# Sharing a PSUM slot between values and transposed values, adding a fourth first-layer slot, and giving pair copies and an eighth of the squares to GpSimd

## The chip, the cores and the metric

The kernel runs on one core of a Trainium2 chip. The metric is the device time of one execution in microseconds (us). A profile also gives the span, the time between the first and the last instruction, which is about 1.7 us shorter than the time (before: span 247.69, time of that run 249.41).

A ratio below is the mean time of a kernel's fast runs over the mean of the fast runs of the kernel before in the same rounds, so it is not quite the ratio of the medians that are quoted beside it. The brackets after a ratio are its 95% interval.

The engines: TensorE (PE in the profile; PEld are its weight loads), VectorE (DVE), ScalarE (ACT), GpSimd (POOL). PSUM, where matmuls write, is used here as two pools: three large slots of two banks and two small slots of one bank.

## The reference, cut to what matters

```python
# attention in chunks of 32 queries; keys: 8 memory keys, 16 left, 32 own, 8 right
for c in range(nc):
    k_full = concatenate([mem_k, k[:, :, l_start:r_end]]);  v_full likewise
    a = exp(scale * q_c @ k_full.T - max);  a = a / sum(a)
    out[:, :, chunk c] = a @ v_full
# then, with x = attention output as (3072 tokens, 512):
h = x @ w_in                              # 512 -> 2048, "first layer"
g = h + sin(alpha * h)**2 / alpha         # alpha per column of w_in
y = g @ w_out                             # 2048 -> 512, "second layer"
```

There are 4 batches of 768 tokens, 8 heads of 64.

Of the kernel before, what the change touches and what calls it, by code (L numbers as in the profile page):

```python
# [9 lines left out]
P = 128  # L10
# [35 lines left out]
def kernel(  # L46
# [154 lines left out]
    nc.scalar.copy(memv_st[64:72], memv_f[64:72])  # L201
# [23 lines left out]
    def pair_up(src, hp):  # L225
        pr = blk.tile([P, 6, 2, D], BF, name="pr")
        nc.vector.tensor_copy(
            pr[:].rearrange("p r e d -> p e r d"), src[:, 2 * hp:2 * hp + 2]
        )
        return pr  # L230
# [52 lines left out]
    def pv(b, j, pt):  # L283
# [15 lines left out]
        return x_blk  # L299

    def xt(xT, j, x_blk):
        xtp = smp.tile([P, KT, QW], BF, name="xtp", tag="sm")
        for kt in range(KT):
            nc.tensor.transpose(  # L304
                xtp[:, kt, :], x_blk[:, 2 * kt:2 * kt + 2, :].rearrange("p e d -> p (e d)"), ident[0:QW, 0:QW]
            )
        nc.vector.tensor_copy(xT[:, :, QW * j:QW * j + QW], xtp[:])  # L307

    def burst(b, stream, shares, lag):
# [3 lines left out]
        for s in range(NJ + lag + 1):  # L313
# [5 lines left out]
            stream.take(n // 2)  # L319
            if 0 <= s - lag < NJ:  # L320
                xbl[s - lag] = pv(b, s - lag, ptl.pop(s - lag))
            stream.take(n - n // 2)
            if 0 <= s - lag - 1 < NJ:
                xt(xT, s - lag - 1, xbl.pop(s - lag - 1))
# [3 lines left out]
    def l1(i, ft, xT, gT, dve_sq):  # L328
        hT = big.tile([P, 2, 512], F32, name="hT", tag="big")
        for kt in range(KT):  # L330
            for hf in range(2):
                nc.tensor.matmul(  # L332
                    hT[:, hf, 0:HALF],
# [5 lines left out]
        nc.scalar.activation(u[:], hT[:, :, 0:HALF], ACTF.Sin, scale=alpha_sb[:, ft:ft + 1])  # L339
        s2 = mlp.tile([P, 2, HALF], F32, name="s2")  # L340
        if dve_sq:
            nc.vector.tensor_tensor(out=s2[:], in0=u[:], in1=u[:], op=ALU.mult)  # L342
        else:
            nc.scalar.activation(s2[:], u[:], ACTF.Square)  # L344
        nc.vector.scalar_tensor_tensor(  # L345
            out=gT[:, ft, :].rearrange("p (e c) -> p e c", e=2),
            in0=s2[:], scalar=inv_alpha[:, ft:ft + 1], in1=hT[:, :, 0:HALF],
            op0=ALU.mult, op1=ALU.add,
        )

    def l2(i, gT, last=False):
        for s in range(NSUB):
            o = smp.tile([P, d_model], F32, name="o", tag="sm")
            for ft in range(FT):
                nc.tensor.matmul(  # L355
                    o[:], gT[:, ft, P * s:P * s + P], w_out_sb[:, ft, :],
                    start=(ft == 0), stop=(ft == FT - 1),
                )
                if ft < FT - 1:
                    yield False  # L360
            o_sb = mlp.tile([P, d_model], F32, name="o_sb")
            if s % 2 == 0:
                nc.vector.tensor_copy(o_sb[:], o[:])  # L363
            else:
                nc.scalar.copy(o_sb[:], o[:])  # L365
            nc.sync.dma_start(out[S * i + P * s:S * i + P * s + P, :], o_sb[:])
            yield True


    prs = [pair_up(kq[n % 2], n // 2) for n in range(2)]  # L370
    for n in range(2 * HP):
        (t_k if n % 2 == 0 else t_q)(prs[n], n // 2)
        spin(2)
        if n + 2 < 2 * HP:
            prs.append(pair_up(kq[n % 2], (n + 2) // 2))
    mt = smp.tile([P, HP, 32], BF, name="mt", tag="sm")
    for hp in range(HP):
        nc.tensor.transpose(mt[:, hp, :], memk_bf[0:32, 2 * hp:2 * hp + 2, :].rearrange("p e d -> p (e d)"), ident[0:32, 0:32])
    nc.vector.tensor_copy(memkT[:], mt[:])
    put_memk(0)  # L380
    put_memv(0)
# [13 lines left out]
    for i in range(B):  # L395
        gT = gp.tile([P, FT, S], BF, name="gT")
        last = i == B - 1
        at_ft = {1: 0, 3: 1, 5: 2, 7: 3, 9: 4, 11: 5, 13: 6, 14: 7}
# [15 lines left out]
        for ft in range(FT):  # L414
            dve_sq = ft % 3 == 1 if i == 0 else ft % 4 == 3
# [4 lines left out]
            l1(i, ft, xT, gT, dve_sq)  # L420
# [3 lines left out]
        if not last:  # L424
# [9 lines left out]
            else:  # L434
                xT = burst(i + 1, stream, (5, 6, 7, 7, 7, 7, 7, 7, 7, 7), 1)
# [37 lines left out]
```

## The kernel before: the parts that the change touches

Each batch goes through an attention of eight blocks of 96 queries, a first layer of 16 tiles (ft), and a second layer of 6 sums. The second layer of one batch is cut into single matmuls (`stream.take(n)` emits up to n of them: it stops where a sum ends and leaves the rest to the next take) that fill TensorE during the next batch's attention and first layer. Batch 0 has nothing to fill with, so its attention has a dummy matmul per block (`spin(1)`).

```python
big = tile_pool(name="big", bufs=3, space=PSUM)      # large slots: sc, ot, hT, z (dummy)
smp = tile_pool(name="smp", bufs=2, space=PSUM)      # small slots: o, xtp, tt_a

def pair_up(src, hp):                                # puts the two heads of a pair side by side
    nc.vector.tensor_copy(pr, src[:, 2*hp:2*hp+2])

def pv(b, j, pt):                                    # values of block j
    ot = big.tile(...)
    # 8 matmuls ot <- pt, vw ; rinv = 1/sum ; x_blk = ot * rinv       (VectorE)
    return x_blk

def xt(xT, j, x_blk):                                # transposed values
    xtp = smp.tile([P, KT, QW], BF, name="xtp", tag="sm")
    # 4 transposes xtp <- x_blk
    nc.vector.tensor_copy(xT[:, :, QW*j:QW*j+QW], xtp[:])

def burst(b, stream, shares, lag):                   # one attention
    for s in range(NJ + lag + 1):
        ptl[s] = qk_exp(s)                           # 8 score matmuls into sc, 3 exponentials
        if b == 0: spin(1)                           # one dummy matmul into a large slot z
        stream.take(n // 2);   xbl[s-lag] = pv(...)
        stream.take(n - n//2); xt(xT, s-lag-1, xbl.pop(s-lag-1))

def l1(i, ft, xT, gT, dve_sq):                       # one first-layer tile
    hT = big.tile(...)                               # 8 matmuls
    u  = sin(alpha * hT)                             # ScalarE
    s2 = u * u                                       # VectorE if dve_sq, else ScalarE
    gT[:, ft] = s2 * inv_alpha + hT                  # VectorE, scalar_tensor_tensor ("STT")
...
for c in range(8): load_w_in(c)                      # all these DMAs are issued by GpSimd,
kq_next = load_qk(1)                                 # in this order
for c in range(4): load_w_out(c)
load_v_all(1)                                        # four loads: values of batch 1
xT = burst(0, stream, (), 2)
...
dve_sq = ft % 3 == 1 if i == 0 else ft % 4 == 3
at_ft = {1: 0, 3: 1, 5: 2, 7: 3, 9: 4, 11: 5, 13: 6, 14: 7}   # key/query transposes, batches 1, 2
```

The softmax here doesn't subtract the row's maximum and nothing guards it: scores larger than these inputs give would overflow.

## Time and profile before

The time before was 250.03 us (median of 3, 249.28 to 250.76). Stages overlap little on TensorE, so I cut the span at the first weight load of each stage, and the end at the end of the last weight load.

| stage (before) | starts at | lasts |
|---|---|---|
| attention 0 | 17.50 | 13.00 |
| first layer 0 and the transposes for batch 1 | 30.50 | 34.67 |
| attention 1 | 65.17 | 16.15 |
| first layer 1 | 81.33 | 31.88 |
| attention 2 | 113.21 | 24.54 |
| first layer 2 | 137.75 | 31.95 |
| attention 3 | 169.70 | 24.67 |
| first layer 3 and last second layer | 194.37 | 49.14 |
| end (last copy and output) | 243.50 | 4.19 |

A timeline line of the profile reads: start, length, engine, line of the kernel, operation, output<-inputs, shapes, count, and in brackets the idle time before it with what ended that idle time. Two pieces of the chain that ended last (start, length, what), between 24 and 32 us, show what led through attention 0 before:

```profile
23.82 1.21 ACT pt L276 x3
31.15 1.31 PE hT L332 x7
```

The chain goes from ScalarE's exponentials over TensorE and VectorE to the first layer's matmuls; no DMA and no GpSimd instruction stands in this part of the chain.

### The profile page before, as it was taken

The numbers are of one execution on the slowest core, as the hardware profiler recorded it, in microseconds if no ns is written. First come the engines' busy times: TensorE is split into PE (matmuls) and PEld (weight loads), VectorE is DVE, ScalarE is ACT, GpSimd is POOL, SyncE is SP. The second block draws the span as 40 slices with busy tenths as digits, with TensorE's granted clock in tenths as the row PEclk, the third lists the DMA queues.
The fourth block names the chain that finished last, engine by engine and source line by source line (L and its number), as shares of the span: only waits on it lengthen the run. The fifth ranks groups of instructions, "written<-read, shape, count | busy, mean of one in ns | idle before, by whom it ended". The sixth has DMA issues, their size and how long they took to land.

```text
span 247.7 us, 4445 instructions
## 1 busy us (share of the span) xinstructions
PE 221.4 (89%) x1769; PEld 122.5 (49%) x1769; DVE 147.0 (59%) x282; ACT 172.3 (70%) x261; POOL 48.1 (19%) x70
## 2 busy tenths in 40 slices
PE   6788788999989998987899997988899999989994
PEld 2345445555445565653455564653455455543441
DVE  3257958897059677675546577776456176575110
ACT  3679678898895797999462798899653687891000
POOL 8899955100900000180000000000000000000000
PEclk9799999999999999999999999999999999999999
DMA  7999999999999700299911101001111101101122
GB/s 79 168 120 70 153 195 204 207 199 118 167 214 154 72 3 12 42 195 143 144 53 42 45 0 42 3 0 42 44 45 43 45 0 42 43 4 42 47 83 85
DMA packets 53709, 21.11 MB, mean 85 GB/s; under 512 B 36280, under 2 KB 50616, under 8 KB 53688
## 3 DMA queue, kind: packets, MB, share of 16 engines
q0 software_dynamic: 47616, 14.40, 72.7%
q1 hardware_dynamic: 6072, 6.43, 8.8%
q8 instruction: 14, 0.23, 0.4%
q14 instruction: 7, 0.06, 0.1%
HBM read 28.91 MB, written 6.29 MB: 142 GB/s over the span
## 4 chain that ended last, share of the span: by engine, by line
PE 55%; ACT 25%; DVE 11%; issue 5%; DMA 2%; SPq 1%; DVEq 0%; ACTq 0%
PE o L355 27%; PE hT L332 18%; ACT u L339 8%; ACT s L344 6%; ACT pt L276 5%; DVE gT L345 3%; PE ot L289 3%; DVE x_blk L294 2%; DMA memv_f<-in_mem_v_dram 2%; PE sc L267 2%; ACT o_sb L365 2%; ACT L276 2%; DVE s L342 2%; PE xtp L304 1%; ACT kTi L244 1%
## 5 line engine op out<-in xcount | busy, mean ns | idle before, releaser
L355 PE MATMUL o<-w_out_sb,gT 128*128 128x512 bf16 x384 | 100.2, 379 | 4.2 <-ACT o_sb L365 1.7
L332 PE MATMUL hT<-xT,w_in_sb 128*128 128x384 bf16 x512 | 91.7, 326 | 4.0 <-DVE gT L345 3.6
L345 DVE SCALAR_TENSOR_TENSOR gT<-s,inv_alpha,hT 128x768 bf16<-128x768 f32 x64 | 64.4, 1013 | 38.2 <-ACT s L344 35.9
L339 ACT ACTIVATE u<-hT,alpha_sb 128x768 f32<-128x768 f32 x64 | 57.3, 897 | 17.1 <-PE hT L332 16.8
L332 PEld LDWEIGHTS <-w_in_sb 128*128 128x128 bf16 x512 | 49.3, 98 | 39.2 <-issue 6.2
L355 PEld LDWEIGHTS <-gT 128*128 128x128 bf16 x384 | 33.9, 97 | 33.3 <-issue 3.9
L276 ACT ACTIVATE pt<-sc,biasm 128x256 bf16<-128x256 f32 x96 | 37.4, 490 | 13.7 <-PE sc L267 13.5
L344 ACT ACTIVATE s<-u 128x768 f32<-128x768 f32 x47 | 39.6, 843 | 1.5
L365 ACT COPY o_sb<-o 128x512 f32<-128x512 f32 x12 | 7.0, 582 | 30.2 <-PE o L355 30.1
L294 DVE TENSOR_TENSOR x_blk<-ot,rinv 96x512 bf16<-96x512 f32 x32 | 22.0, 686 | 1.1
L293 DVE RECIPROCAL rinv<-ot 96x8 f32<-96x8 f32 x32 | 6.4, 199 | 21.6 <-PE ot L289 21.5
L342 DVE TENSOR_TENSOR s<-u 128x768 f32<-128x768 f32 x17 | 16.2, 955 | 2.7 <-ACT u L339 2.6
L289 PEld LDWEIGHTS <-pt 128*128 128x128 bf16 x256 | 11.8, 97 | 10.9 <-ACT pt L276 3.6
L363 DVE COPY o_sb<-o 128x512 f32<-128x512 f32 x12 | 8.2, 687 | 14.4 <-PE o L355 14.3
L171 PE MATMUL z<-zeros 128*128 128x512 bf16 x37 | 14.1, 468 | 2.2 <-DVE zeros L165 1.3
L289 PE MATMUL ot<-vw,pt 128*128 128x65 bf16 x256 | 13.0, 193 | 3.4 <-ACT pt L276 3.0
L307 DVE COPY xT<-xtp 128x384 bf16<-128x384 bf16 x32 | 11.2, 351 | 3.1 <-PE xtp L304 2.0
L267 PE MATMUL sc<-qT,kTi 64*128 64x96 bf16 x256 | 11.0, 205 | 1.8 <-DVE kTi L159 0.8
L304 PEld LDWEIGHTS <-x_blk 96*128 96x128 bf16 x128 | 8.4, 97 | 8.1 <-DVE x_blk L294 2.2
L115 POOL DMA_DIRECT2D k_bf<-in_k_dram x3 | 2.8, 922 | 49.1 <-DVE kTi L250 49.1
L304 PE MATMUL xtp<-ident,x_blk 96*128 96x96 bf16 x128 | 10.8, 206 | 1.3 <-DVE x_blk L294 1.0
L258 PEld LDWEIGHTS <-pr 128*128 128x128 bf16 x96 | 6.5, 99 | 9.2 <-issue 2.3
(53 smaller groups left out, 142.4 us busy)
## 6 DMA issues: line engine op xcount, KB each, us to landing
out_dram<-o_sb SPq DMA_DIRECT2D x24, 256.0 KB, 2.0
k_bf<-in_k_dram POOLq DMA_DIRECT2D x3, 768.0 KB, 8.2
q_bf<-in_q_dram POOLq DMA_DIRECT2D x3, 768.0 KB, 12.0
vw<-in_v_dram POOLq DMA_DIRECT2D x6, 384.0 KB, 15.7
w_in_sb<-in_moe_w_in_dram POOLq DMA_DIRECT2D x8, 256.0 KB, 7.8
w_out_sb<-in_moe_w_out_dram POOLq DMA_DIRECT2D x4, 512.0 KB, 19.0
k_bf<-in_k_dram POOLq DMA_DIRECT2D x4, 192.0 KB, 6.0
q_bf<-in_q_dram POOLq DMA_DIRECT2D x4, 192.0 KB, 6.4
```

The lines of the kernel that those rows point to most:

```text
L171: nc.tensor.matmul(z[:], zeros[:, 0:P], zeros[:])
L267: nc.tensor.matmul(sc[:, e, QW * hp:QW * hp + QW], kTi[64 * e:64 * e + 64, hp, 104 * j:104 * j + P], qT[64 * e:64 * e + 64, hp, QW * j:QW ...
L276: nc.scalar.activation(pt[:, 0:H * QW].rearrange("p (g e c) -> p e g c", g=4, e=2)[:, :, :, 32 * m:32 * m + 32], sc[:, :, 0:4 * QW].rearra ...
L289: nc.tensor.matmul(otv[:, h // 4, h % 4, :], pt[:, QW * h:QW * h + P], vws[b % 2][:, h, j, 0:D + 1])
L294: nc.vector.tensor_tensor(out=x_blk[:].rearrange("p (g e) d -> p g e d", g=2), in0=otv[0:QW, :, :, 0:D], in1=rv.unsqueeze(3).to_broadcast( ...
L304: nc.tensor.transpose(xtp[:, kt, :], x_blk[:, 2 * kt:2 * kt + 2, :].rearrange("p e d -> p (e d)"), ident[0:QW, 0:QW])
L332: nc.tensor.matmul(hT[:, hf, 0:HALF], w_in_sb[:, kt, P * ft:P * ft + P], xT[:, kt, HALF * hf:HALF * hf + HALF], start=(kt == 0), stop=(kt ...
L339: nc.scalar.activation(u[:], hT[:, :, 0:HALF], ACTF.Sin, scale=alpha_sb[:, ft:ft + 1])
L342: nc.vector.tensor_tensor(out=s2[:], in0=u[:], in1=u[:], op=ALU.mult)
L344: nc.scalar.activation(s2[:], u[:], ACTF.Square)
L345: nc.vector.scalar_tensor_tensor(out=gT[:, ft, :].rearrange("p (e c) -> p e c", e=2), in0=s2[:], scalar=inv_alpha[:, ft:ft + 1], in1=hT[:, ...
L355: nc.tensor.matmul(o[:], gT[:, ft, P * s:P * s + P], w_out_sb[:, ft, :], start=(ft == 0), stop=(ft == FT - 1),)
```

## The change

Its intent: take the pair copies off VectorE and a third of the squares off ScalarE, use GpSimd, which is busy for 19% of the span, and free the small PSUM slots so that a second-layer sum need not wait for the last one's copy. Of ScalarE's 47 squares, 8 go to GpSimd and 7 to VectorE. The core of the diff:

```diff
-    def pair_up(src, hp):
+    def pair_up(src, hp, eng=None):
-        nc.vector.tensor_copy(
+        (eng or nc.gpsimd).tensor_copy(            # the first ones still on VectorE
...
-    def xt(xT, j, x_blk):
-        xtp = smp.tile([P, KT, QW], BF, name="xtp", tag="sm")
+    def xt(xT, j, x_blk, ot):                      # ot: the values' slot of the same block
+        xtp = ot[:].bitcast(BF)[:, 0, 640:640 + KT * QW].rearrange("p (k c) -> p k c", k=KT)
...                                                  # burst: takes in three parts, not two, and on past a sum's end
-    def l1(i, ft, xT, gT, dve_sq):
-        hT = big.tile([P, 2, 512], F32, name="hT", tag="big")
+    def l1(i, ft, xT, gT, sq, split=False):
+        if split:                                  # the "fourth slot": the two small ones
+            hts = [smp.tile([P, 512], F32, name="hs", tag="sm") for _ in range(2)]
...                                                  # sine and STT in halves if split
+            (nc.vector if sq == "D" else nc.gpsimd).tensor_tensor(
+                out=s2[:], in0=u[:], in1=u[:], op=ALU.mult)
...
-        at_ft = {1: 0, 3: 1, 5: 2, 7: 3, 9: 4, 11: 5, 13: 6, 14: 7}
+        at_ft = {2 * n: n for n in range(8)}
-            dve_sq = ft % 3 == 1 if i == 0 else ft % 4 == 3
+            sq = ("ADAPADAD" if i == 0 else "ADAPADAD")[ft % 8]
-            l1(i, ft, xT, gT, dve_sq)
+            l1(i, ft, xT, gT, sq, i == 0 and ft % 4 == 3)
-                xT = burst(i + 1, stream, (5, 6, 7, 7, 7, 7, 7, 7, 7, 7), 1)
+                xT = burst(i + 1, stream, (9, 9, 7, 6, 6, 6, 6, 6, 6, 5), 1)
```

In "ADAPADAD" A is ScalarE, D VectorE, P GpSimd. Cut here: the last second-layer sum comes out in two halves, and the steps that prepare the memory keys and values come in another order at the start.

More of the change, by code (lines that the diff above doesn't have):

```diff
@@ L200 @@
     nc.scalar.copy(memk_bf[:], memk_f[:])
-    nc.scalar.copy(memv_st[64:72], memv_f[64:72])
     for j in range(NJ):
@@ L298, in pv @@
         )
-        return x_blk
-    def xt(xT, j, x_blk):
-        xtp = smp.tile([P, KT, QW], BF, name="xtp", tag="sm")
+        return x_blk, ot
+    def xt(xT, j, x_blk, ot):
+        xtp = ot[:].bitcast(BF)[:, 0, 640:640 + KT * QW].rearrange("p (k c) -> p k c", k=KT)
         for kt in range(KT):
@@ L306, in xt @@
             )
-        nc.vector.tensor_copy(xT[:, :, QW * j:QW * j + QW], xtp[:])
+        nc.vector.tensor_copy(xT[:, :, QW * j:QW * j + QW], xtp)
     def burst(b, stream, shares, lag):
@@ L318, in burst @@
                 spin(1)
-            stream.take(n // 2)
+            stream.take(n // 3, True)
             if 0 <= s - lag < NJ:
                 xbl[s - lag] = pv(b, s - lag, ptl.pop(s - lag))
-            stream.take(n - n // 2)
+            stream.take((n + 1) // 3, True)
             if 0 <= s - lag - 1 < NJ:
-                xt(xT, s - lag - 1, xbl.pop(s - lag - 1))
-        return xT
-    def l1(i, ft, xT, gT, dve_sq):
-        hT = big.tile([P, 2, 512], F32, name="hT", tag="big")
+                xt(xT, s - lag - 1, *xbl.pop(s - lag - 1))
+            stream.take((n + 2) // 3, True)
+        return xT
+    def l1(i, ft, xT, gT, sq, split=False):
+        if split:
+            hts = [smp.tile([P, 512], F32, name="hs", tag="sm") for _ in range(2)]
+        else:
+            hT = big.tile([P, 2, 512], F32, name="hT", tag="big")
+            hts = [hT[:, 0], hT[:, 1]]
         for kt in range(KT):
@@ L332, in l1 @@
                 nc.tensor.matmul(
-                    hT[:, hf, 0:HALF],
+                    hts[hf][:, 0:HALF],
                     w_in_sb[:, kt, P * ft:P * ft + P],
@@ L338, in l1 @@
         u = mlp.tile([P, 2, HALF], F32, name="u")
-        nc.scalar.activation(u[:], hT[:, :, 0:HALF], ACTF.Sin, scale=alpha_sb[:, ft:ft + 1])
+        if split:
+            for hf in range(2):
+                nc.scalar.activation(
+                    u[:, hf], hts[hf][:, 0:HALF], ACTF.Sin, scale=alpha_sb[:, ft:ft + 1])
+        else:
+            nc.scalar.activation(u[:], hT[:, :, 0:HALF], ACTF.Sin, scale=alpha_sb[:, ft:ft + 1])
         s2 = mlp.tile([P, 2, HALF], F32, name="s2")
-        if dve_sq:
-            nc.vector.tensor_tensor(out=s2[:], in0=u[:], in1=u[:], op=ALU.mult)
-        else:
-            nc.scalar.activation(s2[:], u[:], ACTF.Square)
-        nc.vector.scalar_tensor_tensor(
-            out=gT[:, ft, :].rearrange("p (e c) -> p e c", e=2),
-            in0=s2[:], scalar=inv_alpha[:, ft:ft + 1], in1=hT[:, :, 0:HALF],
-            op0=ALU.mult, op1=ALU.add,
-        )
+        if sq == "A":
+            nc.scalar.activation(s2[:], u[:], ACTF.Square)
+        else:
+            (nc.vector if sq == "D" else nc.gpsimd).tensor_tensor(
+                out=s2[:], in0=u[:], in1=u[:], op=ALU.mult)
+        gv = gT[:, ft, :].rearrange("p (e c) -> p e c", e=2)
+        for hf in range(2):
+            if split:
+                nc.vector.scalar_tensor_tensor(
+                    out=gv[:, hf], in0=s2[:, hf], scalar=inv_alpha[:, ft:ft + 1],
+                    in1=hts[hf][:, 0:HALF], op0=ALU.mult, op1=ALU.add)
+            elif hf == 0:
+                nc.vector.scalar_tensor_tensor(
+                    out=gv, in0=s2[:], scalar=inv_alpha[:, ft:ft + 1],
+                    in1=hT[:, :, 0:HALF], op0=ALU.mult, op1=ALU.add)
     def l2(i, gT, last=False):
@@ L353, in l2 @@
             o = smp.tile([P, d_model], F32, name="o", tag="sm")
-            for ft in range(FT):
-                nc.tensor.matmul(
-                    o[:], gT[:, ft, P * s:P * s + P], w_out_sb[:, ft, :],
-                    start=(ft == 0), stop=(ft == FT - 1),
-                )
-                if ft < FT - 1:
-                    yield False
-            o_sb = mlp.tile([P, d_model], F32, name="o_sb")
-            if s % 2 == 0:
-                nc.vector.tensor_copy(o_sb[:], o[:])
-            else:
-                nc.scalar.copy(o_sb[:], o[:])
-            nc.sync.dma_start(out[S * i + P * s:S * i + P * s + P, :], o_sb[:])
+            end = last and s == NSUB - 1
+            o_sb = mlp.tile([P, d_model], F32, name="o_sb")
+            row = S * i + P * s
+            if end:
+                oh = [o, smp.tile([P, d_model], F32, name="o", tag="sm")]
+                for c in range(2):
+                    cs = slice(256 * c, 256 * c + 256)
+                    for ft in range(FT):
+                        nc.tensor.matmul(
+                            oh[c][:, 0:256], gT[:, ft, P * s:P * s + P], w_out_sb[:, ft, cs],
+                            start=(ft == 0), stop=(ft == FT - 1),
+                        )
+                    if c == 0:
+                        nc.scalar.copy(o_sb[:, cs], oh[c][:, 0:256])
+                    else:
+                        nc.vector.tensor_copy(o_sb[:, cs], oh[c][:, 0:256])
+                    nc.sync.dma_start(out[row:row + P, cs], o_sb[:, cs])
+            else:
+                for ft in range(FT):
+                    nc.tensor.matmul(
+                        o[:], gT[:, ft, P * s:P * s + P], w_out_sb[:, ft, :],
+                        start=(ft == 0), stop=(ft == FT - 1),
+                    )
+                    if ft < FT - 1:
+                        yield False
+                if s % 2 == 0:
+                    nc.vector.tensor_copy(o_sb[:], o[:])
+                else:
+                    nc.scalar.copy(o_sb[:], o[:])
+                nc.sync.dma_start(out[row:row + P, :], o_sb[:])
             yield True
-    prs = [pair_up(kq[n % 2], n // 2) for n in range(2)]
+    prs = [pair_up(kq[n % 2], n // 2, nc.vector) for n in range(2)]
     for n in range(2 * HP):
@@ L373 @@
         spin(2)
-        if n + 2 < 2 * HP:
-            prs.append(pair_up(kq[n % 2], (n + 2) // 2))
-    mt = smp.tile([P, HP, 32], BF, name="mt", tag="sm")
-    for hp in range(HP):
-        nc.tensor.transpose(mt[:, hp, :], memk_bf[0:32, 2 * hp:2 * hp + 2, :].rearrange("p e d -> p (e d)"), ident[0:32, 0:32])
-    nc.vector.tensor_copy(memkT[:], mt[:])
-    put_memk(0)
-    put_memv(0)
+        if n == 1:
+            nc.scalar.copy(memv_st[64:72], memv_f[64:72])
+            mt = smp.tile([P, HP, 32], BF, name="mt", tag="sm")
+            for hp in range(HP):
+                nc.tensor.transpose(
+                    mt[:, hp, :],
+                    memk_bf[0:32, 2 * hp:2 * hp + 2, :].rearrange("p e d -> p (e d)"),
+                    ident[0:32, 0:32])
+        if n + 2 < 2 * HP:
+            prs.append(pair_up(kq[n % 2], (n + 2) // 2, nc.vector))
+        if n == 1:
+            nc.vector.tensor_copy(memkT[:], mt[:])
+            put_memk(0)
+        if n == 3:
+            put_memv(0)
     put_memv(1)
```

## The prediction

> **What bounds the kernel now.** I read the page first (busy shares, slices), then the groups, then the waits and the timeline stage by stage. The page:
>
> ```profile
> PE 221.4 (89%) x1769; PEld 122.5 (49%) x1769; DVE 147.0 (59%) x282; ACT 172.3 (70%) x261; POOL 48.1 (19%) x70
> ...
> PEclk9799999999999999999999999999999999999999
> DMA  7999999999999700299911101001111101101122
> ```
>
> TensorE is the bound on average, but its shortfall differs by stage. POOL looks free (19%), which is what invites the change; nearly all of that is DMA issue in the first 48 us, while the DMA engines are full (slices 2 to 13). The groups whose counts the change alters:
>
> ```profile
> L345 DVE SCALAR_TENSOR_TENSOR gT<-s,inv_alpha,hT 128x768 bf16<-128x768 f32 x64 | 64.4, 1013 | 38.2 <-ACT s L344 35.9
> L339 ACT ACTIVATE u<-hT,alpha_sb 128x768 f32<-128x768 f32 x64 | 57.3, 897 | 17.1 <-PE hT L332 16.8
> L344 ACT ACTIVATE s<-u 128x768 f32<-128x768 f32 x47 | 39.6, 843 | 1.5
> L342 DVE TENSOR_TENSOR s<-u 128x768 f32<-128x768 f32 x17 | 16.2, 955 | 2.7 <-ACT u L339 2.6
> ```
>
> Each first-layer tile (ft) costs TensorE 1.30 us (8 matmuls), ScalarE a sine, some engine a square, VectorE one scalar_tensor_tensor (STT). Stages from the timeline: batch 0's attention to 31.1 us, its first layer to 55.4, transposes with second layer to 65.2, attention 1 to 81.5, first layer 1 to 113.2, attention 2 to 138.0, and so on; the last second layer ends at 244. In attention 2 the waits that the change aims at show directly:
>
> ```profile
> 117.21 0.42 PE L289 MATMUL ot<-vw,pt 128*128 128x65 bf16 x8 [1.44 <-ACT pt L276]
> ...
> 121.16 1.24 PE L355 MATMUL o<-w_out_sb,gT 128*128 128x512 bf16 x5 [0.73 <-DVE o_sb L363]
> ...
> 126.49 0.81 PE L355 MATMUL o<-w_out_sb,gT 128*128 128x512 bf16 x3 [0.22 <-ACT o_sb L365]
> ...
> 136.67 1.46 PE L355 MATMUL o<-w_out_sb,gT 128*128 128x512 bf16 x6 [0.50 <-ACT o_sb L365]
> ```
>
> The brackets are TensorE idle: the next second-layer sum can't start until the last is copied out, because the transposed values hold the other small PSUM slot. The lines on which my prediction turns are GpSimd's own timeline:
>
> ```profile
> 38.86 1.33 POOL L142 DMA_DIRECT2D vw<-in_v_dram  x1
> 42.68 0.78 POOL L145 DMA_DIRECT2D vw<-in_v_dram  x1 [2.49 <-DMA k_bf<-in_k_dram]
> 46.58 0.83 POOL L148 DMA_DIRECT2D vw<-in_v_dram  x1 [3.12 <-DMA q_bf<-in_q_dram]
> ```
>
> GpSimd stands in its queue until 47.4 us: its DMA issues reuse eight semaphores, so the last load of batch 1's values waits until the queries of batch 1 have landed (46.6).
>
> **What the Trainium skill says.** GPSIMD Engine Reference, section 3.1, gives a two-input fp32 elementwise operation of 2048 elements 4497 ns, about 2.2 ns an element; for 768 I estimate 1.7 to 1.8 us. The trace before has no such operation. TensorE: Matmul & The Clock Gate, Part 1, calls GpSimd's queue strictly first in first out and says that TensorE falls to half clock after an idle window of some 3.4 us. The trace agrees with the half clock: slice 2 shows 0.7, which is 3.4 us at half within 6.2. SBUF — State Buffer, "Who interferes with whom": a VectorE instruction with two SBUF inputs and a GpSimd instruction that reads SBUF exclude each other for the whole instruction. VectorE's squares are of that kind; the trace before cannot show it.
>
> **The change part by part.** All times are on the clock of the trace before.
>
> *Batch 0, squares on GpSimd.* In the changed build the square of ft 3 stands on GpSimd directly behind the last value load, so it starts at 47.4 at the earliest and, with 1.8 us, ends at 49.2. Its sine is done at about 38. VectorE runs in order, so from STT 2 (about 38.5) it idles until 49.2; TensorE fills the slots of ft 4 to 6 and stops at about 41. Then I walk ft 3 to 15 with durations from the rows above: STT start to start 0.93, a VectorE square with its STT 2.0, half an STT 0.6, half a sine 0.6 (both worked out from the fixed part of short instructions on that engine), 1.30 for TensorE. VectorE is the bound: STT 3 to 50.4, STT 6 starts 53.3, STT 7 ends 56.4, STT 10 ends 60.3, a wait of 0.65 for GpSimd's square of ft 11, STT 11 ends 62.1, STT 14 starts 65.0, the halves of STT 15 end at 67.6 and 68.1.
>
> *The fourth slot.* It is the two small PSUM slots. ft 15 lies there too, and the first transposes of the next batch take the same slot: in the build they wait for VectorE. So TensorE, which finishes ft 15 at 63.5, idles to 67.6. Before, those transposes began at 55.37. Delay 12.25, plus 0.25 because the first second-layer sum waits for the second half. Even without the wait at ft 3 this bubble would cost about 3.5 (two half sines, square, half STT).
>
> *Clock.* TensorE idles some 9 us and later 4 us. One window of 3.4 us at half clock after each loses up to 1.7; the first is partly beside VectorE's backlog. I count 1.5 in all. Pair copies and VectorE's square of ft 13 exclude each other: 0.5.
>
> *Transposed values in the slot of the values.* The slot of a block's values is held one block longer, so the three large slots rotate differently. The build's bank addresses show that in steady state every score tile takes the same slot as the one before it, so it waits for the exponentials of the block just before. A block's three exponentials take 1.21; score to exponential takes 0.39 (23.43 to 23.82) and the semaphore 0.06, so a chained block takes 1.66. Attention 0: five blocks, +1.8, but it ends before 47.4 and vanishes in the wait. Attention 1: exponentials ran 67.18 to 76.82, 9.64; new 5 x 1.21 + 3 x 1.66 = 11.0, so +1.4, less 0.3 for a transpose group now inside the stage. Attention 2 and 3 need 2.07 of TensorE per block (6 second-layer matmuls at 0.216, scores 0.28, values 0.24, transposes 0.26), more than 1.66, so the chain hides.
>
> *Gains.* Attention 2 and 3: the waits 0.73, 0.22 and 0.50 go; nine instead of five matmuls before the first values take 0.5 off the 1.44; some shorter gaps: 2.2 each, 4.4. First layers 1 and 2: ScalarE had 16 x 0.90 + 12 x 0.84 + 8 x 0.75 + 0.6 = 31.1 us of work in a stage of 31.7 us; with 8 squares it has 27.7, and TensorE's 29 becomes the bound; with two slow squares and the exclusion I count 1.2 each, 2.4. Moved memory keys and values at the start: hidden. First layer 3: the square of ft 11 on GpSimd lengthens a slot's cycle from about 4.3 to 5.2 where no second-layer work fills in: -0.3. Last output in halves: a shorter copy and DMA, 0.4.
>
> Sum: 12.25 + 0.25 + 1.5 + 0.5 + 1.1 + 0.3 - 4.4 - 2.4 - 0.4 = +8.7, so 258.7 from 250.03. The clock and the backlog may overlap, so I take 258.
>
> **The rivals.** (1) The wait at ft 3 does not bind: the queries of batch 1 land before 40 us, or TensorE has enough to do meanwhile. Then the losses are the bubble at ft 15 (3.5) and the two chains (1.8 + 1.1), less about 1.5 for the extra slot and 6.9 for the later gains: about 248. Against it: DMA is at 9 in every slice up to there, the loads are unchanged in number and order, and GpSimd's wait names q_bf. (2) GpSimd is much slower than estimated, or the exclusion hits every VectorE square: each of 24 pair copies and 8 squares then delays VectorE by up to 1 us, first layers 1 to 3 gain nothing and batch 0 loses 2 more: 262 to 264. For it: only the skill's figure for one two-input operation is known. Against it: in first layers 1 and 2 VectorE has 23 us of work in 30. (3) Attention 2 and 3 also fall to the slot chain: were the score tile to wait 0.4 per block, 3 us each would be lost and the total be near 264. Against it: 2.07 exceeds 1.66.
>
> **Range and chances.** Rival 1 I give 0.15, rival 2 0.15, rival 3 0.05. The rest lies around 258, with 2 us either way from the later gains and 1.5 from the clock. The 2% limits are 245.0 and 255.0. Range 252 to 263; faster 0.04, within 2% 0.21, slower 0.75.
>
> **What would show each step right or wrong.** Right: GpSimd's first square starts at 46 to 48 us; VectorE's idle before the halves of ft 3 is about 10 us, put down to POOL; TensorE has idles of 8 to 10 us before ft 7 and about 4 us before the first transposes of batch 1, and PEclk dips after the first; from the fourth or sixth block of attention 0 and 1 ScalarE idles 0.4 us before each block's exponentials, for the scores; the waits of o on o_sb are gone in attention 2 and 3, and each is about 2 us shorter; the ScalarE square group falls to 32 instructions, first layers 1 and 2 take about 30.5. The prediction is wrong if GpSimd reaches its first square before about 42 us, if a GpSimd square takes much over 2 us, or if first layers 1 and 2 shrink by 3 us each.

## The result, and the profile after

The changed kernel took 259.02 us (median of 4, 257.44 to 259.86) against 249.73 (median of 4, 249.28 to 250.76): ratio 1.0359 [1.0298, 1.0419], so slower. The page after, first the busy times, then the granted clock and the DMA share in 40 slices of 6.4 us:

```profile
PE 224.8 (87%) x1758; PEld 125.9 (49%) x1785; DVE 147.7 (57%) x270; ACT 162.2 (63%) x250; POOL 80.4 (31%) x102
...
PEclk9998589779899999999999999999999999999999
DMA  8999999999109993010599910010111201010222
```

The work did move: ScalarE lost 10.1 us, POOL gained 32.3. TensorE's clock is down in slices 4 to 6 (counted from 1), at 0.5 in slice 5 (26 to 32 us, attention 0), at 0.7 in slices 8 and 9 (45 to 58 us), and at 0.8 in slice 11 (64 to 71 us). The groups:

```profile
L353 POOL TENSOR_TENSOR s<-u 128x768 f32<-128x768 f32 x8 | 11.7, 1467 | 87.0 <-ACT u L348 75.6
L351 ACT ACTIVATE s<-u 128x768 f32<-128x768 f32 x32 | 27.0, 844 | 1.3 <-DVE gT L358 0.3
...
L226 POOL COPY pr<-q_bf 128x768 bf16<-128x768 bf16 x12 | 10.6, 882 | 43.9 <-PE tt_a L242 33.8
```

A square takes GpSimd 1.47 us, where ScalarE took 0.84 and VectorE 0.96; ScalarE has 32 squares left of 47, VectorE 24 in place of 17. Now the timeline of the changed kernel in first layer 0, the lines of several engines put in order of time:

```profile
42.99 0.78 POOL L145 DMA_DIRECT2D vw<-in_v_dram  x1 [2.23 <-DMA k_bf<-in_k_dram]
46.89 0.83 POOL L148 DMA_DIRECT2D vw<-in_v_dram  x1 [3.12 <-DMA q_bf<-in_q_dram]
47.74 1.48 POOL L353 TENSOR_TENSOR s<-u 128x768 f32<-128x768 f32 x1
49.26 1.14 DVE L358 SCALAR_TENSOR_TENSOR gT<-s,inv_alpha,hs 128x384 bf16<-128x384 f32 x2 [5.64 <-POOL s L353]
49.92 1.32 PE L336 MATMUL hs<-xT,w_in_sb 128*128 128x384 bf16 x3 [4.27 <-DVE gT L358]
...
62.16 1.14 DVE L358 SCALAR_TENSOR_TENSOR gT<-s,inv_alpha,hs 128x384 bf16<-128x384 f32 x2 [1.10 <-POOL s L353]
...
68.85 0.80 PE L242 MATMUL tt_a<-ident,pr 128*128 128x128 bf16 x6 [4.20 <-DVE gT L358]
```

Read it downwards. GpSimd waits with a value load for the queries of batch 1 to land (3.12), then issues it, and only then squares tile 3. VectorE had been idle for 5.64 us for this square, TensorE for 4.27. The last line is the second stop: the first transposes for batch 1 need the small slots in which tile 15 lies, and wait 4.20 us for VectorE to finish with it. They start 13.5 us later than before (55.37). The chain that ended last says the same:

```profile
29.40 13.30 DMA k_bf<-in_k_dram
43.77 3.10 issue
47.74 1.49 POOL s L353
```

A DMA of 13.30 us, GpSimd's queue and its square now lead, beside attention 0, into first layer 0. Attention 0 itself is not on this path, although it became longer: its block period rose, as ScalarE's exponentials show in the timeline after,

```profile
25.32 1.21 ACT L275 ACTIVATE pt<-sc,biasm 128x256 bf16<-128x256 f32 x3 [1.15 <-PE sc L266]
27.84 1.21 ACT L275 ACTIVATE pt<-sc,biasm 128x256 bf16<-128x256 f32 x3 [1.31 <-PE sc L266]
```

(a block every 2.52 us) against before, where nine exponentials of three blocks ran as one piece of 3.78:

```profile
23.82 3.78 ACT L276 ACTIVATE pt<-sc,biasm 128x256 bf16<-128x256 f32 x9 [0.28 <-PE sc L267]
```

In attention 2, where the prediction showed four waits of TensorE, the timeline after has one left over 0.2 us between the stage's first matmul and first layer 2:

```profile
133.06 0.42 PE L288 MATMUL ot<-vw,pt 128*128 128x65 bf16 x8 [0.64 <-ACT pt L275]
```

The whole balance, stage by stage, is the length after minus the length before:

| part | predicted | measured |
|---|---|---|
| start of attention 1 | +14.5 | +14.86 |
| attention 1 | +1.1 | +1.55 |
| first layer 1 | -1.2 | -0.62 |
| attention 2 | -2.2 | -2.24 |
| first layer 2 | -1.2 | -0.97 |
| attention 3 | -2.2 | -2.65 |
| first layer 3 with last second layer | +0.3 | +0.46 |
| end | -0.4 | -0.74 |
| sum (span 257.34 - 247.69) | +8.7 | +9.65 |

### The profile page after: what moved, and what is told of

Its sections match the earlier page's. It is cut to its first block, busy times and chain, and to the rows that moved or that the text cites. A ratio compares the mean times of both kernels' runs of the same rounds, so it can differ in the third digit from the quotient of the medians.

```text
span 257.3 us, 4477 instructions
## 1 busy us (share of the span) xinstructions
PE 224.8 (87%) x1758; PEld 125.9 (49%) x1785; DVE 147.7 (57%) x270; ACT 162.2 (63%) x250; POOL 80.4 (31%) x102
## 4 chain that ended last, share of the span: by engine, by line
PE 55%; POOL 12%; ACT 11%; DVE 8%; issue 7%; DMA 5%; POOLq 1%; ACTq 0%; DVEq 0%
PE o L388 24%; PE hT L336 21%; DMA k_bf<-in_k_dram 5%; ACT u L348 3%; ACT pt L275 3%; POOL vw L125 3%; DVE gT L362 2%; POOL vw L129 2%; POOL w_in_sb L212 2%; PE ot L288 2%; ACT s L351 2%; PE tt_a L242 2%; DVE x_blk L293 2%; PE sc L266 2%; ACT L275 1%
## 5 line engine op out<-in xcount | busy, mean ns | idle before, releaser
L388 PE MATMUL o<-w_out_sb,gT 128*128 128x512 bf16 x342 | 94.1, 382 | 1.7 <-DVE gT L362 0.4
L336 PE MATMUL hT<-xT,w_in_sb 128*128 128x384 bf16 x480 | 86.8, 329 | 1.6 <-DVE gT L362 1.2
L362 DVE SCALAR_TENSOR_TENSOR gT<-s,inv_alpha,hT 128x768 bf16<-128x768 f32 x60 | 60.3, 1012 | 34.2 <-ACT s L351 23.3
L336 PEld LDWEIGHTS <-w_in_sb 128*128 128x128 bf16 x512 | 50.0, 99 | 42.0 <-issue 10.1
L353 POOL TENSOR_TENSOR s<-u 128x768 f32<-128x768 f32 x8 | 11.7, 1467 | 87.0 <-ACT u L348 75.6
L351 ACT ACTIVATE s<-u 128x768 f32<-128x768 f32 x32 | 27.0, 844 | 1.3 <-DVE gT L358 0.3
L353 DVE TENSOR_TENSOR s<-u 128x768 f32<-128x768 f32 x24 | 24.2, 1009 | 0.6 <-ACT u L348 0.5
L226 POOL COPY pr<-q_bf 128x768 bf16<-128x768 bf16 x12 | 10.6, 882 | 43.9 <-PE tt_a L242 33.8
L243 ACT COPY kTi<-tt_a 128x672 bf16<-128x672 bf16 x11 | 7.9, 716 | 9.9 <-PE tt_a L242 9.8
L266 PEld LDWEIGHTS <-kTi 64*128 64x128 bf16 x256 | 7.3, 97 | 12.0 <-issue 6.1
L303 PE MATMUL ot<-ident,x_blk 96*128 96x96 bf16 x128 | 11.6, 217 | 1.4 <-DVE x_blk L293 1.4
```

Of the source, the lines that this page charges most:

```text
L266: nc.tensor.matmul(sc[:, e, QW * hp:QW * hp + QW], kTi[64 * e:64 * e + 64, hp, 104 * j:104 * j + P], qT[64 * e:64 * e + 64, hp, QW * j:QW ...
L336: nc.tensor.matmul(hts[hf][:, 0:HALF], w_in_sb[:, kt, P * ft:P * ft + P], xT[:, kt, HALF * hf:HALF * hf + HALF], start=(kt == 0), stop=(kt ...
L351: nc.scalar.activation(s2[:], u[:], ACTF.Square)
L353: (nc.vector if sq == "D" else nc.gpsimd).tensor_tensor(out=s2[:], in0=u[:], in1=u[:], op=ALU.mult)
L362: nc.vector.scalar_tensor_tensor(out=gv, in0=s2[:], scalar=inv_alpha[:, ft:ft + 1], in1=hT[:, :, 0:HALF], op0=ALU.mult, op1=ALU.add)
L388: nc.tensor.matmul(o[:], gT[:, ft, P * s:P * s + P], w_out_sb[:, ft, :], start=(ft == 0), stop=(ft == FT - 1),)
```

## The experiments

My theory after the result: batch 0 loses by two causes that partly hide each other, the GpSimd square that stands behind a load in its queue and the fourth slot; attentions 0 and 1 lose by the shared slot; attentions 2 and 3 gain by it. Rivals: GpSimd is just too slow for squares; and one of the two causes in batch 0 explains all of it. Then I asked what the gains of batches 1 to 3 come of. Twelve kernels ran, all correct.

| run | what it is | time, us | ratio to before |
|---|---|---|---|
| e1 | changed kernel, no GpSimd squares in batch 0 | 254.96 | 1.0225 [1.0168, 1.0281] |
| e2 | changed kernel, no fourth slot | 256.60 | 1.0268 [1.0228, 1.0308] |
| e3 | both of these | 250.74 | 1.0052 [1.0014, 1.0089] |
| e4 | e3, and no shared slot in attentions 0 and 1 | 244.28 | 0.9781 [0.9753, 0.9809] |
| e5 | changed kernel, batch 1's value loads issued later | 254.79 | 1.0188 [1.0156, 1.0219] |
| e6 | e3, three dummies per block | 250.30 | 1.0025 [1.0001, 1.0048] |
| e7 | e4, no GpSimd squares at all | 243.01 | 0.9737 [0.9709, 0.9764] |
| e8 | e4, all pair copies on VectorE | 247.69 | 0.9923 [0.9900, 0.9947] |
| e9 | e7, two more things as before | 242.00 | 0.9681 [0.9657, 0.9705] |
| e10 | e3, dummy in a small slot | 246.93 | 0.9896 [0.9868, 0.9925] |
| e11 | kernel before with the shared slot and its takes in attentions 2 and 3 | 243.49 | 0.9753 [0.9728, 0.9778] |
| e12 | e7, squares dealt out as before | 244.90 | 0.9801 [0.9780, 0.9823] |

The kernel before took 249.47 in the rounds of e1 to e4, 249.55 in those of e5 to e8 and 249.71 in those of e9 to e12 (medians). Lengths of the stages in us, cut as above ("layer 0" includes the transposes for batch 1):

| stage | before | after | e3 | e4 | e7 | e11 | e12 | e9 |
|---|---|---|---|---|---|---|---|---|
| attention 0 | 13.00 | 18.67 | 18.67 | 13.34 | 13.34 | 12.99 | 13.34 | 13.35 |
| layer 0 | 34.67 | 44.13 | 35.75 | 35.58 | 35.42 | 34.68 | 34.73 | 34.93 |
| attention 1 | 16.15 | 17.70 | 17.70 | 16.95 | 16.95 | 16.15 | 16.95 | 16.64 |
| layer 1 | 31.88 | 31.26 | 31.26 | 31.26 | 30.93 | 31.89 | 31.80 | 30.94 |
| attention 2 | 24.54 | 22.30 | 22.30 | 22.30 | 22.24 | 21.75 | 22.53 | 22.25 |
| layer 2 | 31.95 | 30.99 | 30.99 | 30.99 | 30.66 | 31.46 | 31.53 | 30.67 |
| attention 3 | 24.67 | 22.02 | 22.01 | 22.01 | 21.95 | 21.96 | 22.25 | 21.96 |
| layer 3 | 49.14 | 49.59 | 49.59 | 49.59 | 49.07 | 49.14 | 49.39 | 49.07 |

### e1, e2, e3: the two causes in batch 0, singly and together

e1 changes one string, e2 one argument, e3 does both.

```diff
-            sq = ("ADAPADAD" if i == 0 else "ADAPADAD")[ft % 8]
+            sq = ("ADAAADAD" if i == 0 else "ADAPADAD")[ft % 8]          # e1, e3
-            l1(i, ft, xT, gT, sq, i == 0 and ft % 4 == 3)
+            l1(i, ft, xT, gT, sq, False)                                 # e2, e3
```

> Edit: in batch 0 alone, the squares of ft 3 and 11 go to ScalarE instead of GpSimd; the split slot, the shared PSUM slot and all other GpSimd work stay. Theory (GpSimd's square queues behind the DMA issues): VectorE's 5.6 us idle before the halves of ft 3 goes, the first layer of batch 0 starts at about 36 us as in the changed kernel, and the first transposes of batch 1 come at about 64.5 instead of 68.9 us, still after a bubble of about 4 us; time about 254.5 (minus 4.5). Rival (the loss is GpSimd's pair copies and squares slowing VectorE everywhere): two of 32 GpSimd operations fewer, at most 1 us less, 258.

> Edit: the fourth slot is not used (no split tile in batch 0); the GpSimd square of ft 3 stays and still waits for the DMA issues. Theory (the transposes of batch 1 wait for the last split tile): TensorE's idle of 4.2 us before the first transposes goes, VectorE's idle before ft 3 of batch 0 stays at 5 to 6 us; time about 254.5 (minus 4.5). If the bubble only showed VectorE's backlog and the second layer has to wait for it anyway, the time falls by less than 1.5 us, 257.5 or more.

> Edit: both of the last two edits: no GpSimd square in batch 0 and no split tile. Theory: nothing hides attention 0's longer time any more (it ends at 35.9 instead of 30.5 us), first layer 0 takes about 24.5 us, attention 1 begins at about 70.3 us (80.0 in the changed kernel, 65.2 in the kernel before), time about 249.2. If the gains of the two edits were independent and additive the time would be about 250; if one hid the other, about 254.

The waits (engine and output, releaser, us in total, times, longest) between 36 and 82 us, of e1:

```profile
PE tt_a L242 <- DVE gT L358: 3.6, 1, 3.6
```

and of e2:

```profile
DVE gT L362 <- POOL s L353: 7.1, 2, 5.7
```

Each undoing leaves the other's wait in place. With the medians: GpSimd's squares cost 259.02 - 254.96 = 4.1 with the fourth slot and 256.60 - 250.74 = 5.9 without it; the fourth slot costs 2.4 with the squares and 4.2 without. Together 8.3, more than 4.1 + 2.4, so each cause hides part of the other. My reading is that TensorE's extra tile in the fourth slot is done beside VectorE's backlog; that is argued from the waits, not run. e2 came between its two expectations; e1 came as the theory said, and e3 1.5 us above it.

e3 also shows VectorE and GpSimd hindering each other, in two meetings of a VectorE square with a pair copy on GpSimd:

```profile
63.02 0.95 DVE L353 TENSOR_TENSOR s<-u 128x768 f32<-128x768 f32 x1
63.38 1.28 POOL L226 COPY pr<-k_bf 128x768 bf16<-128x768 bf16 x1 [0.37 <-PE tt_b L257]
...
100.92 0.83 POOL L226 COPY pr<-k_bf 128x768 bf16<-128x768 bf16 x1 [0.52 <-PE tt_a L257]
100.98 1.57 DVE L353 TENSOR_TENSOR s<-u 128x768 f32<-128x768 f32 x1
```

Undisturbed they take 0.95 and 0.82. The one that starts first keeps its length, the other is drawn out, to 1.28 or 1.57. This agrees with the section of the Trainium skill that the prediction drew on (SBUF — State Buffer, "Who interferes with whom"), which says that the order of issue decides who blocks. A third square, at 46.90, took 1.45 although the pair copy beside it started later, at 47.43. A DMA issue of GpSimd ran just before that copy, from 46.60 to 47.43; what drew this square out stays open, since other squares beside such issues kept their 0.95. Such meetings are rare: the VectorE squares of e4 average 1.017 over 24, those of e8 (no GpSimd copies) 0.952, 1.6 us in all over the run.

### e4: without the shared slot in attentions 0 and 1

```diff
-        return x_blk, ot
+        return (x_blk, ot) if b >= 2 else (x_blk, None)      # None: xt takes a small slot, as before
```

> Edit: as the last one, and in the attention of batches 0 and 1 the transposed values have their own small PSUM slot again, as in the kernel before; batches 2 and 3 keep the shared slot. Theory (the slot held longer makes each score tile wait for the exponentials of the block before): ScalarE's idles of 1.2 to 1.3 us per block in attention 0 go, TensorE's clock stays full there, attention 0 takes 13 us again instead of 18.7 and attention 1 16.2 instead of 17.7; time about 242.3, faster than both kernels. Rival (attention 0 is longer because memory keys and values and their copies moved into the start): attention 0 stays at 18 us, time 248 to 249.

It took 244.28 and is faster than both kernels. Attention 0 falls back to 13.34, so the moved memory keys and values, the rival, are not what lengthened it. My 242.3 was missed by 2 us: attention 1 came to 16.95 and not to 16.2, and e3, from which I had counted, was itself 1.5 us slower than expected.

### e5: the same GpSimd square, another place in the queue

```diff
-    load_v_all(1)
...
+            if i == 0 and ft == 4:
+                load_v_all(1)
```

> The changed kernel whole, its two GpSimd squares of batch 0 kept, but the four loads of batch 1's values are issued between the first-layer tiles 3 and 4 of batch 0 instead of before the attention. Theory (place in the queue): GpSimd's square of tile 3 then waits for its sine alone and starts at about 42 to 43 us instead of 47.7, VectorE's wait of 5.6 us before tile 3 falls to about 1.5, and the time falls by about 4, to 255 (as in the run without GpSimd squares in batch 0, 254.96). Rival (GpSimd too slow, whatever stands before it): the wait stays above 4 us and the time at 258 or more. Second rival: the loads now land too late for attention 1, or their issues hold up a later pair copy: 255 is missed with a new wait for vw or pr.

Its timeline:

```profile
44.91 1.47 POOL L353 TENSOR_TENSOR s<-u 128x768 f32<-128x768 f32 x1 [8.01 <-ACT u L345]
...
46.41 1.14 DVE L358 SCALAR_TENSOR_TENSOR gT<-s,inv_alpha,hs 128x384 bf16<-128x384 f32 x2 [1.32 <-POOL s L353]
```

The square takes about as long as before, 1.47, but waits for its sine alone, and VectorE waits 1.32 in place of 5.64. At 254.79 the kernel is as fast as with no GpSimd squares in batch 0 (e1, 254.96). So the loss of 4 us was the place in the queue, not GpSimd's speed. The start, 44.91, was later than I expected (42 to 43), because this run reached tile 3's sine later: the 24 matmuls of its first three tiles took 5.80 us, partly at half clock, where the changed kernel took about 4.5.

### e6, e10: why attention 0 grew by 5.67 and not by 1.8

e3 is the base, since there attention 0 is on the path.

```diff
             if b == 0:
-                spin(1)
+                spin(3)             # e6
+                spin(1, True)       # e10: z in a small slot in place of a large one
```

> The kernel e3 (250.74: neither GpSimd squares in batch 0 nor the fourth slot, shared slot still in attention 0), with three instead of one dummy matmul per block of attention 0. Theory: the slot chain by itself makes a block about 1.7 to 1.9 us, and the rest of the 2.52 comes of TensorE at half clock, to which the idle of the chain let it fall. With 0.43 us more of work per block the clock should stay up, a block should take about 1.9, and attention 0 should last 14 to 16 us instead of 18.67: about 247 to 248. Rival: the clock only follows the chain and adds nothing; then attention 0 stays at 18.7 or grows by up to 0.4 a block: 250.5 to 254.

My expectation for e6 failed. Its clock was full in every slice, and attention 0 still lasted 18.56. The timeline line that repeats in each block of e6:

```profile
26.27 0.81 PE L171 MATMUL z<-zeros 128*128 128x512 bf16 x2 [0.83 <-DVE xT L306]
```

The dummy waits for VectorE's copy of the transposed values. So the slow clock had not made the period; it came with it. The same chain in the changed kernel's timeline:

```profile
26.45 0.60 PE L288 MATMUL ot<-vw,pt 128*128 128x65 bf16 x8
27.08 0.20 DVE L292 RECIPROCAL rinv<-ot 96x8 f32<-96x8 f32 x1 [1.33 <-PE ot L288]
27.32 0.69 DVE L293 TENSOR_TENSOR x_blk<-ot,rinv 96x512 bf16<-96x512 f32 x1
27.93 0.34 DVE L306 COPY xT<-ot 128x384 bf16<-128x384 bf16 x1
28.32 0.59 PE L171 MATMUL z<-zeros 128*128 128x512 bf16 x1 [0.52 <-DVE xT L306]
```

Values at 26.45, reciprocal and x_blk behind them in VectorE's queue, the copy that frees the shared slot behind those, and at 28.32 the dummy, which takes that slot; the next values start at 28.96. That is the period of 2.5 us. What e6 could not tell is how much the two extra dummies lengthened this chain while the full clock shortened it. e10 takes the dummy out of the rotation:

> Kernel e3 (250.74), one change: the one dummy matmul per block of attention 0 writes to a small PSUM slot, which nothing else uses there, instead of a large one. The run with three dummies showed a full clock and still 18.56 us for attention 0, with every dummy waiting 0.83 us for VectorE's copy of the transposed values (DVE xT). Theory now: the dummy is the wait. Its large slot is the one that holds values and transposed values of the block before, so TensorE, which runs in order, stops at the dummy until that copy is done, and values, transposes and the next scores come behind it. With the dummy elsewhere a block should take about 1.5 instead of 2.52, attention 0 should last 14 to 15.5 us instead of 18.67, and the time be 246 to 247.5. Rival (the prediction's: scores wait for the exponentials of the block before, whatever the dummy does): a block takes 1.66 to 1.9 at full clock or stays at 2.5 at half clock, and attention 0 lasts 16.5 us or more: 248.5 to 251.

```profile
26.21 1.21 ACT L276 ACTIVATE pt<-sc,biasm 128x256 bf16<-128x256 f32 x3 [0.43 <-PE sc L267]
27.85 1.21 ACT L276 ACTIVATE pt<-sc,biasm 128x256 bf16<-128x256 f32 x3 [0.43 <-PE sc L267]
```

Attention 0 lasts 15.43 and the time is 246.93, both as the new theory said; but the period is 1.64, not 1.5, which is the prediction's own figure of 1.66 with its idle of 0.43. Both chains exist: the shared slot costs 15.43 - 13.34 = 2.1 by the scores that wait for the block before, and the dummy's slot 18.67 - 15.43 = 3.2 more. The clock is not parted from these sizes: its mean over attention 0 was 0.73 in e3, 0.89 in e10 and full in e4. But e6 shows that the dummy's slot holds attention 0 near 18.6 at full clock too.

### e7, e12, e8: what GpSimd and the squares do in batches 1 to 3

```diff
-            sq = ("ADAAADAD" if i == 0 else "ADAPADAD")[ft % 8]                # e4
+            sq = ("ADAAADAD" if i == 0 else "ADAAADAD")[ft % 8]                # e7
+            sq = "AD"[ft % 3 == 1] if i == 0 else "AD"[ft % 4 == 3]            # e12
-        (eng or nc.gpsimd).tensor_copy(
+        (eng or nc.vector).tensor_copy(                                        # e8
```

> The kernel e4 (244.28), with the two GpSimd squares of each of batches 1 to 3 given to ScalarE, so that GpSimd does no square at all. Theory of the prediction (ScalarE's load bounds the first layers 1 and 2): ScalarE gets 1.7 us more in each, 26.2 to 27.9 in 31.2, as before the change, and first layers 1 and 2 go back by 0.3 to 0.5 each, while first layer 3 wins 0.3 because the slow square of tile 11 goes: 244.5 to 245.0. Rival: the squares on GpSimd bring nothing, and what the first layers gained came of other things: 243.8 to 244.2, with first layers 1 and 2 unchanged within 0.15.

Neither expectation held: 243.01, 1.3 less than e4. First layers 1 and 2 shorten by 0.33 each and layer 3 by 0.52, although ScalarE has more to do. GpSimd's squares cost time in every batch. In e4 VectorE waits for them 2.7 us in first layer 1 (two waits, the longest 1.4); in e7 such waits are gone.

> Kernel e7 (243.01), with the squares dealt out as before the change: every third on VectorE in batch 0, every fourth in batches 1 to 3, the rest on ScalarE. ScalarE gets two more squares (1.7 us) in each of batches 1 to 3, VectorE two fewer. Theory of the prediction (ScalarE's load bounds first layers 1 and 2): they go from 30.93 and 30.66 back towards 31.9, by 0.5 to 0.9 each, while first layer 0 wins 0.5: 243.5 to 244.5. Rival (the first layers gained by the pair copies on GpSimd and the earlier transposes, not by the squares): first layers 1 and 2 stay within 0.25, and the time is 242.3 to 243.1.

244.90, a little over the range of the theory. Layers 1 and 2 go back by 0.87 each. The busy times of first layer 1 (window, length, then PE, PEld, DVE, ACT, POOL, each with its count, clock, DMA share, GB/s), of e7:

```profile
83.00:113.93 30.93, 29.24 (x199) 17.56 (x200) 21.16 (x29) 27.48 (x34) 13.27 (x14) 1.00 0.76 80
```

and of e12:

```profile
82.20:114.00 31.80, 29.55 (x199) 17.48 (x199) 19.32 (x27) 28.73 (x36) 13.70 (x14) 1.00 0.69 75
```

Two squares moved between ScalarE and VectorE, 1.25 us of ScalarE's time and 1.84 of VectorE's; TensorE's work changes by 0.31. So the two squares are worth 0.87 on VectorE in place of ScalarE, which fits the prediction's view that ScalarE's load holds these stages. It is not shown to be the cause: even in e12 ScalarE idles 3.07 of the 31.80, and the dealing also changes at which tiles the VectorE squares come, which no run parts from their number.

> The kernel e4 (244.28), with all pair copies back on VectorE (16 GpSimd copies of 0.9 us in batches 1 and 2 and 8 in batch 0 become VectorE copies of 0.36 to 0.4). Theory: VectorE has 21.7 us of work in a first layer of 31.2, so 3 more are hidden, and GpSimd gives nothing back but its exclusion: the time within 0.5 of 244.3, with first layers 1 and 2 within 0.3. Rival (copies in VectorE's queue delay the results that TensorE's slots wait for): each first layer longer by 0.5 or more, 245.3 or more. Second rival (exclusion by GpSimd costs): each shorter by 0.3 or more, 243.5 or less.

247.69: the rival's time, but not its place. The loss is not in the first layers (+0.19 each) but at the ends of attentions 1 (+1.73) and 2 (+1.30). The timeline of e8 at the end of attention 1:

```profile
84.25 0.36 DVE L226 COPY pr<-k_bf 128x768 bf16<-128x768 bf16 x1
...
84.67 0.51 PE L242 MATMUL tt_a<-ident,pr 128*128 128x128 bf16 x6 [1.56 <-DVE pr L226]
```

The change also moves the first transposes from tile 1 to tile 0. On VectorE the pair copy then stands behind the last copies of the attention, TensorE waits 1.56 us for it, and the first layer comes after. On GpSimd it is ready in time. With the old order of transposes (e11) attention 1 lasts 16.15 with the pair copies on VectorE, as before. No run has the new order undone alone.

### e11: the shared slot and its takes alone; e9: the best version

e11 is the kernel before with the `xt` of the change in attentions 2 and 3 (as in e4), its three-part takes and its shares there, and nothing else.

> The kernel before, with one part of the change alone: in attentions 2 and 3 the transposed values lie in the slot of the values, and the second-layer matmuls are spread as the change spreads them. Nothing on GpSimd, no other squares, no fourth slot. Theory: the gain of attentions 2 and 3 is the slot's alone, 2.24 and 2.65, and first layers stay as before (31.9 within 0.2): 249.5 - 4.9 = 244.6, within 0.7. Rival (part of the gain needs the pair copies off VectorE, which then delay x_blk and xT): the two stages win under 3.5 in all, 246 or more.

243.49: better than I expected. Attentions 2 and 3 win 2.79 and 2.71, first layer 1 nothing, first layer 2 0.50. This part alone is worth 2.5%. It holds two things that no run parts: the slot, and the takes, which run on past the end of a sum and come earlier (9, 9, 7 in place of 5, 6, 7). In e12, too, batches 2 and 3 have both; besides them it has GpSimd's pair copies with the new order of transposes, attention 1's new takes, the new start and the halved last sum, and it is 1.4 us slower than e11. So these together cost time.

e9 is e7 with batch 0's squares and attention 1's takes as before.

> A version put together from what the runs showed: kernel e7 (243.01: shared slot in attentions 2 and 3 alone, no fourth first-layer slot, no GpSimd squares, pair copies on GpSimd), and in batch 0 and attention 1 two more things as before the change: the squares of batch 0 (every third on VectorE) and the number of second-layer matmuls between the steps of attention 1. Theory: each stage keeps its better form, so first layer 0 goes from 25.24 back to about 24.7 and attention 1 from 16.95 to about 16.15, and the time is 243.0 - 0.5 - 0.8 = 241.7. Rival: the later start of something else takes it up, and it stays at 242.5 to 243.

242.00, ratio 0.9681, the fastest kernel. Layer 0 came to 34.93 and attention 1 to 16.64, a little short of the 16.15 hoped for, since a group of transposes now stands inside that stage. Every slice of its page has a clock of 9.

## Why the prediction was right, point by point

The prediction was right: 258.0 against 259.02, and slower, to which it gave 0.75. The main mechanism was right as well. That the sum came so near is partly luck: attention 0 was three times off but hidden, and in attention 1 and the first layers terms were wrong, some of them in sign.

**The wait at tile 3** was the main term and held: the first GpSimd square started at 47.74 (predicted 47.4 or later), VectorE's halves of tile 3 ended at 50.4 as predicted, and e1 and e5 show that this square and its place in the queue cost about 4 us. Its length was off, 1.47 in place of 1.8. What did not hold is the picture around it: VectorE idled 5.64 and not 10 us, TensorE 4.27 and not 8 to 10. Attention 0 ended 5.4 us later than before, so both engines came later to a wait whose end was fixed by a DMA. The start of attention 1 moved by 14.86 against 14.5 for just that reason.

**The bubble at tile 15** held: predicted 3.5 by itself, e1 against e3 gives 4.2; in the changed kernel TensorE idled 4.20 where the walk through the tiles has 63.5 to 67.6. The walk ended 1.2 us early (69.33 for the last half against 68.1). Of the exclusion (0.5) the trace shows 0.15: the square of tile 13 took 1.10, behind a pair copy. The clock's 1.5 was not measured singly. The trace has the clock at half from 48.09 to 54.91 and again from 68.56 to 71.98, so after both waits, for 6.8 and 3.4 us where the prediction had 3.4 each.

**Attention 0, "+1.8"**, is the mis-sized term. Its mechanism is real and exact (1.64 per block in e10, 2.1 in all), but the dummy matmuls take slots from the same three, and a dummy that waits for VectorE's copy holds everything behind it: 3.2 more. That it "vanishes in the wait" was right in the changed kernel, and would have cost nearly the whole 5.7 in a kernel without the wait: e3 against e4 shows 5.33. Rival 1 of the prediction (no wait at tile 3, but the bubble: 248) is what e1 makes of it, and e1 took 254.96. The larger part of the gap is this term: in e1 attention 0 is on the path and lasts 19.39, 6.4 more than before in place of 1.8.

**First layers 1 and 2, "1.2 each"**, brought 0.62 and 0.97; the layers last 31.26 and 30.99, not 30.5. The prediction summed single durations to 31.1 us of work for ScalarE; the trace before has ScalarE busy for 27.80 of the 31.88 of first layer 1, in part since the records of consecutive instructions overlap. So ScalarE was not as full as it thought. The runs part the gain. For layer 1: two squares from ScalarE to VectorE -0.87 (e12 to e7), two more from ScalarE to GpSimd +0.33 (e7 to e4), pair copies on GpSimd with the earlier transposes -0.09 (e11 to e12), slot and takes alone 0.01: -0.62. For layer 2: -0.87, +0.33, +0.07, and -0.49 by the slot and takes: -0.96. So the step "with two slow squares and the exclusion I count 1.2" failed in one sign: giving ScalarE's squares to GpSimd cost, it did not gain. There is also a wait that I had not foreseen, in the middle of first layer 1 in the timeline after: a group of transposes now lies behind a second-layer sum whose copy is not done.

```profile
114.14 0.49 PE L242 MATMUL tt_a<-ident,pr 128*128 128x128 bf16 x6 [1.63 <-DVE o_sb L395]
```

It is in every run with the new order of transposes (1.6 us in e4, e7, e8 and e12) and in neither with the old one (before, e11), so it lies inside the -0.09. In that same step another group of transposes leaves first layer 1 for attention 1, and yet the layer hardly gains.

**Attentions 2 and 3, "2.2 each"**, brought 2.24 and 2.65. e11 gives the slot with its takes 2.79 and 2.71: some half a microsecond of attention 2 is given back in the changed kernel, about the 0.5 us of TensorE for the transposes that the change moves from tile 1 into this stage. The latter is argued from the schedule, not run.

**Layer 3 and the end**: +0.46 against +0.3, of which GpSimd's squares are +0.52 (e7 to e4), the other dealing of squares -0.32 (e12 to e7), and the rest +0.25; the end -0.74 against -0.4. Attention 1 was +1.55 against +1.1, by other terms: the prediction had +1.4 for the shared slot and -0.3 for a group of transposes. The wait is there (ScalarE idles 0.43 before two of the last three blocks), but e4 gives the slot only 0.75. The new takes cost 0.31 (e7 to e9), and the 0.49 that e9 still has over the kernel before is about what the group of transposes inside the stage takes, so a cost and not a gain; that last step is not run alone.

## What to carry to other kernels

Before work is given to an engine that looks idle, look at what stands in its queue at that moment: here a square of 1.5 us cost 4 us because it stood behind a load that waited for another load, and moving the load mended it (e5). When a buffer is held longer, go through everything that takes a turn in the same rotation, fillers and dummies too, since an in-order engine stops at the first of them that waits. And run the parts of a bundle alone: the shared slot with its takes in the later attentions was worth 2.5% (e11), while the bundle lost 3.6%.

## What the Trainium skill lacked or had wrong

- GPSIMD Engine Reference, section 3.1: the only measured figure of the section for a two-input operation is 2048 fp32 elements, 2.2 ns an element. Here 768 elements with the same tile as both inputs took 1.467 us on average over 8, or 1.9 ns an element with all fixed cost in it. The section has no figure for a bf16 copy; the pair copies of 768 elements took 0.88 us on average, 0.82 where nothing met them.
- TensorE: Matmul & The Clock Gate, Part 1: its table ties the half clock to a whole idle window of about 3.4 us. The same part tells of a kernel whose frequent micro-idles made the clock swing ("A second HAM failure mode"), but says neither how long they were nor how busy TensorE was. In attention 0 of the changed kernel the clock was at half from 24.19 us on, although no idle of TensorE in the 8 us before exceeded 0.8 us; TensorE was busy for 1.84 of the last 3.41 us. In e6, with 2.32 of the same 3.41 us (20.78 to 24.19), the clock stayed full. So part-time work did not keep the clock up here; where the limit lies was not measured.
